# Attention scores by products over 64 rows, a tile's two key halves side by side on the two row halves of TensorE

## Chip, cores and metric

The kernel runs on one core of one Trainium2 chip. The metric is the device time of one execution in microseconds (us); lower is better. TensorE (PE in the profile) multiplies matrices into PSUM, its weight loads are listed as PEld, VectorE is DVE, ScalarE is ACT, GpSimd is POOL, and SyncE (SP) issues nearly all DMAs here.

## What is computed

Attention over 2 batches of 8 heads, 576 positions, 64 numbers per head, then two expert layers on the 1152 token rows of 512 numbers:

```python
q_rot, k_rot = (rotate(q), rotate(k))               # rotary embedding on both
scores = scale * np.matmul(q_rot, k_rot.transpose(0, 1, 3, 2))
scores = scores - np.max(scores, axis=-1, keepdims=True)
attn = np.exp(scores)
attn = attn / (np.sum(attn, axis=-1, keepdims=True) + 1e-09)
return np.matmul(attn, v).astype(np.float32)
# then x = heads side by side, (1152, 512)
x = elu(x @ w_in) @ w_out          # 512 -> 2048 -> 512
x = (h * tanh(softplus(h))) @ w2_out   where h = x @ w2_in
```

## The kernel before

**Numbers in two parts.** Products are made in the fp32r format. Each factor is split into a high part (`qh`, `kh`, ...) and the rest (`ql`, `kl`, ...), and a product is the sum of three: high by high, low by high, high by low.

**Attention.** The 16 heads are worked as 8 pairs (`p`); a pair's two heads lie on partitions 0 to 63 and 64 to 127. A pair has 9 units (`u = 9 p + i`). Units 0 to 7 are a tile each: one head `h`, 128 queries `t`. Unit 8 takes the last 64 queries of both heads at once, with block-diagonal weights `bh`, `bl` over all 128 rows. A unit's 576 scores lie in two PSUM banks, 288 keys (`HS`) in each (`j` = 0, 1).

`do_S(u)` makes the scores, `do_max` their extreme on DVE, `do_exp` the exponentials `P` on ACT. Three units later (`LAG`) `do_T` transposes `P` on PE into `psT`, 128x128 each (L481), with the leftover columns going into `psL` (L486, L483); DVE or ACT copies them to `pt`. `do_av` multiplies by the values with weights of 64 columns (L521, into `psA`). `do_spread` (L458, L462) turns the row sums on PE. There are two score buffers (`ps_s`), so a unit's scores wait for `do_exp` of two units before.

**Scores, first and second pair (`p < FLAT`).** Two units, one of each head, go together: a head's rows 0 to 63 or 64 to 127 alone are contracted (forms "64\*128 64x288" in the profile), three passes by two key halves by two heads, 12 matmuls, with the two heads' alternating.

**Scores, third to eighth pair.** A tile contracts all 128 rows. `ka` holds a head's high keys on rows 0 to 63 and low keys on rows 64 to 127; `qa` holds the high queries on both halves, `qb` the low queries on rows 0 to 63 and zeros below. `qa` by `ka` and `qb` by `ka`, for two key halves, are four matmuls "128\*128 128x288". `spread` makes these stacked tiles by DMAs on SP's queue from `kh`, `kl`, `qh`, `ql`, one pair ahead.

**Order.** The order of the work is written out by hand in one loop over `u`. In units 0 to 8 of a pair, what PE does right before `do_S` is: unit 0 `psL`; 1 `do_av`; 2 `psL`; 3 `do_spread` (L458, L462); 4 `do_av`; 5 `psL`; 6 `do_av`; 7 `do_spread` (L458); 8 `do_av`. Right behind `do_S` come the transposes `psT` of unit `u - 3`. Preparation of pair `p + 1` (rotation, splitting on POOL, the DMAs of `stack_k` and `stack_q`) is spread over pair `p`'s units; in the last two pairs, parts of the expert layers' weight preparation (L96 to L127) stand between the units.

**Expert layers.** `g1_mm` (L187) multiplies by the first weights, L777 and L801 by the second; the weights are turned from 64-bit floats to high and low parts on POOL, DVE and ACT as they come in.

Of the kernel before, what the change touches and what calls it, by code (L numbers as in the profile page):

```python
# [11 lines left out]
F32R = mybir.dt.float32r  # L12
# [9 lines left out]
def plain(ap):  # L22
    return ap.bitcast(F32)
# [3 lines left out]
def kernel(  # L27
# [11 lines left out]
    nc = tc.nc  # L39
    NP = qk.shape[0]  # L40
    S = qk.shape[3]
    HS = S // 2
# [11 lines left out]
    TPP = 9  # L54
# [118 lines left out]
    def ps_s():  # L173
        i = s_count[0]
        s_count[0] += 1
        if s_more[0] is not None and i % 3 == 2:
            return s_more[0].tile([128, 2, 512], F32, tag="s2", name="ps_s2", bufs=1)
        return s_pool.tile([128, 2, 512], F32, tag="s", name="ps_s", bufs=2)
# [67 lines left out]
    def attention(att, ps, tail):  # L246
# [11 lines left out]
        FLAT = 2  # L258
# [48 lines left out]

        def split_alloc(p):
            d = {}
            for nm in ("kh", "kl", "ql"):  # L310
                d[nm] = att.tile([128, S], F32R, tag=nm, name=nm, bufs=2)
            for nm in ("qa",) if p < FLAT else ("ka", "qa"):
                d[nm] = att.tile([128, 2, S], F32R, tag=nm, name=nm, bufs=2)
            d["qh"] = d["qa"][:, 0, :] if p < FLAT else att.tile([128, S], F32R, tag="qh", name="qh", bufs=1)
            i = p % 2
            d["qb"] = qb[i]
            d["bh"], d["bl"] = bd[i]
            sp_t[p] = d

        def split_half(p, i, h, l):  # L320
# [26 lines left out]
                in1=plain(d[h][:, cs]), op0=ALU.mult, op1=ALU.subtract,  # L347
            )

        def spread(dst, src, r):  # L350
            for h in range(2):
                nc.sync.dma_start(out=plain(dst[64 * r:64 * r + 64, h, :]), in_=plain(src[64 * h:64 * h + 64, :]))

        def stack_k(p):
            d = sp_t[p]
            spread(d["ka"], d["kh"], 0)
            spread(d["ka"], d["kl"], 1)

        def stack_q(p):
            d = sp_t[p]  # L360
            for r in range(0 if p < FLAT else 2):
                spread(d["qa"], d["qh"], r)
            if p >= FLAT:
                spread(d["qb"], d["ql"], 0)
            for r in range(2):
                sl = slice(64 * r, 64 * r + 64)
                nc.sync.dma_start(out=plain(d["bh"][sl, 64 * r:64 * r + 64]), in_=plain(d["qh"][sl, S - 64:S]))
                nc.sync.dma_start(out=plain(d["bl"][sl, 64 * r:64 * r + 64]), in_=plain(d["ql"][sl, S - 64:S]))

        tiles = [(h, t) for t in range(4) for h in range(2)] + [None]  # L370
        psS = {}
# [8 lines left out]
        def do_S(u):  # L380
            p, i = divmod(u, TPP)
            d = sp_t[p]
            if p < FLAT and i < TPP - 1:
                us = (u, u + 1) if i % 2 == 0 else ()
            else:
                us = (u,)
            work = []
            for w in us:
                psS[w] = ps_s()
                if tiles[w % TPP] is None:  # L390
                    work.append([
                        (d["bh"], lambda ks: d["kh"][:, ks]),
                        (d["bh"], lambda ks: d["kl"][:, ks]),
                        (d["bl"], lambda ks: d["kh"][:, ks]),
                    ])
                    continue
                h, t = tiles[w % TPP]
                cols = slice(128 * t, 128 * t + 128)
                if p < FLAT:
                    rows = slice(64 * h, 64 * h + 64)  # L400
                    work.append([
                        (d["qh"][rows, cols], lambda ks, rows=rows: d["kh"][rows, ks]),
                        (d["ql"][rows, cols], lambda ks, rows=rows: d["kh"][rows, ks]),
                        (d["qh"][rows, cols], lambda ks, rows=rows: d["kl"][rows, ks]),
                    ])
                else:
                    work.append([
                        (d["qa"][:, h, cols], lambda ks: d["ka"][:, h, ks]),
                        (d["qb"][:, h, cols], lambda ks: d["ka"][:, h, ks]),
                    ])  # L410
            for a in range(len(work[0]) if work else 0):
                for j in range(2):
                    for w, passes in zip(us, work):
                        l, r = passes[a]
                        nc.tensor.matmul(  # L415
                            psS[w][:, j, :HS], lhsT=l, rhs=r(slice(j * HS, j * HS + HS)),
                            start=(a == 0), stop=(a == len(passes) - 1),
                        )

        def do_max(u):  # L420
            m = att.tile([128, 16], F32, tag="mn", name="mn", bufs=4)[:, 0:1]
# [142 lines left out]
        bd = []  # L564
        for i in range(2):
            pair = []
            for nm in ("bh", "bl"):
                t = att.tile([128, 128], F32R, name=f"{nm}{i}")
                nc.vector.memset(plain(t), 0.0)
                pair.append(t)  # L570
            bd.append(pair)
        qb = [att.tile([128, 2, S], F32R, name=f"qb{i}") for i in range(2)]
        for t in sums:
            nc.vector.memset(t[:, :, 1:2], 1e-9)
        nc.vector.memset(pl_t[1][S - 512:128, 256:384], 0.0)
        for t in qb:
            nc.gpsimd.memset(plain(t[64:128]), 0.0)
        nc.gpsimd.memset(halves, 0.0)
        for h in range(2):
            nc.gpsimd.memset(halves[64 * h:64 * h + 64, 64 * h:64 * h + 64], 1.0)  # L580
        nc.gpsimd.tensor_tensor(out=twice, in0=idn[:, 0:64], in1=idn[:, 64:128], op=ALU.add)
        split_alloc(0)
        def keep_warm(n):
            for _ in range(n):
# [19 lines left out]
        def prepare(p, k):  # L604
            if k == 0:
                if p == 2:
                    load_pair(3)
                split_alloc(p)
                split_half(p, 2, "kh", "kl")
                stack_k(p)  # L610
            elif k == 1:
                split_half(p, 0, "qh", "ql")
                stack_q(p)
            elif p + 1 < NP:
                rope_part(p + 1, 2 if k < 5 else 0, (k - 2) % 3, nc.gpsimd)
# [26 lines left out]
        for u in range(max(av_at) + 1):  # L642
            p, i = divmod(u, TPP)
# [3 lines left out]
            if u == 2:  # L647
                load_pair(2)
                split_alloc(1)
# [17 lines left out]
            if u < NU:  # L667
                do_S(u)
# [16 lines left out]
            if u == 2:  # L685
                first_lo(*HEAD[-1])
                stack_q(0)
# [20 lines left out]
            if 0 <= u - LAG < NU:  # L708
                j = (u - LAG) % TPP
# [21 lines left out]
            if u == 7:  # L731
                stack_q(1)
# [176 lines left out]
    with tc.tile_pool(name="att", bufs=1, reuse_waits="tile") as att, tc.tile_pool(  # L909
        name="ps_att", bufs=1, space=bass.MemoryType.PSUM, reuse_waits="tile"  # L910
    ) as ps:
        with tc.manual_schedule():
            attention(att, ps, tail)
# [56 lines left out]
```

## Time and profile before

| | us |
|---|---|
| median of 3 runs | 559.64 |
| lowest and highest run | 558.6, 561.39 |
| span of the profiled execution, first to last instruction | 559.2 |

The profiled execution's own time outside its span is not listed; its span is 0.4 below the median of the runs. Attention lies in the first 160 us, the third to eighth pair's scores between 47.6 and 144.5 us of it. Times of the views are microseconds from the span's start. Matmuls are pipelined: one takes about 0.3 us from its start to its end, and the next one starts well before that, so that the distance of two starts is what one costs.

### The profile page before, as it was taken

Reading aid. Unit: us, or ns where it says so; the run is one execution under the profiler, and the core shown is the slowest. Engines: PE = TensorE matmul, PEld = TensorE weight load, DVE = VectorE, ACT = ScalarE, POOL = GpSimd, SP = SyncE. Lnnn points to the kernel's source line nnn. Section 1 sums busy time; section 2 is a strip of 40 time slices with the busy share of each in tenths; the row PEclk is TensorE's granted clock in tenths of the full one; section 3 lists DMA queues with packets and bytes.
Section 4 is the critical chain, followed back from the end, with each engine's and each line's share of the span. In section 5 each row is a group of like instructions: output and inputs, shape, how many; then the busy total and the mean of one; then the engine's idle time right before and its main releaser. Section 6 shows DMA issues by size and latency. Waiting matters only on the chain.

```text
span 559.2 us, 8818 instructions
## 1 busy us (share of the span) xinstructions
PE 546.1 (98%) x3328; PEld 500.5 (90%) x3328; DVE 375.8 (67%) x560; ACT 267.4 (48%) x459; POOL 244.4 (44%) x227
## 2 busy tenths in 40 slices
PE   7889999999999999999999999999999999999997
PEld 6667878888898999999999999999989989989985
DVE  4868777879867888888889878857336555521221
ACT  3746666677656675554554556344342233132120
POOL 7979898953315434434334531534414433310000
PEclk9979999999999999999999999999999999999999
DMA  7379778764331333323232321423222131000012
GB/s 234 106 208 222 184 207 215 198 140 144 88 114 42 113 113 111 112 78 93 96 112 76 114 76 38 139 88 114 84 105 90 62 114 43 34 0 1 38 39 94
DMA packets 49258, 59.82 MB, mean 107 GB/s; under 512 B 20928, under 2 KB 39104, under 8 KB 48448
## 3 DMA queue, kind: packets, MB, share of 16 engines
q1 hardware_dynamic: 48672, 58.67, 35.6%
q8 instruction: 26, 0.43, 0.3%
q10 hardware_dynamic: 544, 0.59, 0.3%
q14 instruction: 16, 0.13, 0.1%
HBM read 47.51 MB, written 2.36 MB: 89 GB/s over the span
## 4 chain that ended last, share of the span: by engine, by line
PE 87%; DVE 3%; POOL 3%; issue 3%; DMA 2%; ACT 1%; SPq 0%; POOLq 0%; ACTq 0%
PE ps_s L187 33%; PE ps_h L801 18%; PE ps_g L777 17%; PE ps_s L415 7%; PE psA L521 7%; PE psT L481 4%; DMA qk_t<-in_qk_dram 1%; DVE mn L422 1%; DMA bh<-qa 1%; ACT P L435 1%; POOL wu L96 1%; POOL wo0bl L127 1%; POOL wo0l L127 1%; PE psL L486 0%; DVE wu L108 0%
## 5 line engine op out<-in xcount | busy, mean ns | idle before, releaser
L100 DVE TENSOR_SCALAR wu<-wu 128x512 int32<-128x512 int32 x64 | 39.7, 620 | 43.1 <-POOL wu L96 43.1
L759 ACT ACTIVATE ta<-ps_s 128x768 f32<-128x768 f32 x24 | 19.5, 812 | 100.8 <-PE ps_s L187 100.8
L422 DVE TENSOR_REDUCE mn<-ps_s 128x1 f32<-128x576 f32 x72 | 53.5, 752 | 21.0 <-PE ps_s L415 20.8
L435 ACT ACTIVATE P<-ps_s,mn 128x576 f32<-128x576 f32 x72 | 53.1, 740 | 14.7 <-DVE mn L422 14.3
L104 DVE SCALAR_TENSOR_TENSOR wu<-raw,wu 128x512 int32<-128x512 int32 x64 | 50.6, 791 | 2.0
L187 PE MATMUL ps_s<-XH,wi0h 128*128 128x384 f32 x192 | 49.1, 336 | 0.0
L108 DVE SCALAR_TENSOR_TENSOR wu<-raw,wu 128x512 int32<-128x512 int32 x64 | 47.8, 747 | 1.8
L187 PE MATMUL ps_s<-XL,wi1h 128*128 128x384 f32 x192 | 48.9, 335 | 0.0
L187 PE MATMUL ps_s<-XL,wi0h 128*128 128x384 f32 x192 | 48.8, 335 | 0.0
L187 PE MATMUL ps_s<-XH,wi1l 128*128 128x384 f32 x192 | 48.8, 335 | 0.0
L187 PE MATMUL ps_s<-XH,wi0l 128*128 128x384 f32 x192 | 48.8, 335 | 0.0
L187 PE MATMUL ps_s<-XH,wi1h 128*128 128x384 f32 x192 | 48.7, 334 | 0.0
L96 POOL TENSOR_SCALAR wu<-raw 128x512 f32<-128x512 f32 x64 | 46.4, 728 | 4.3
L127 POOL TENSOR_TENSOR wi0l<-wu,wi0h 128x512 fp32r<-128x512 f32 x16 | 23.0, 1440 | 57.5 <-ACT wi0h L126 57.5
L127 POOL TENSOR_TENSOR wi1l<-wu,wi1h 128x512 fp32r<-128x512 f32 x16 | 24.3, 1523 | 54.1 <-ACT wi1h L126 54.1
L127 POOL TENSOR_TENSOR wo1l<-wu,wo1h 128x512 fp32r<-128x512 f32 x16 | 23.3, 1462 | 48.6 <-ACT wo1h L126 48.6
L481 PE MATMUL psT<-idn,P 128*128 128x128 f32 x288 | 43.7, 276 | 0.0
L761 DVE TENSOR_TENSOR g<-ta,g 128x768 fp32r<-128x768 f32 x16 | 17.5, 1093 | 37.0 <-ACT g L760 37.0
L501 ACT ACTIVATE pt<-psT 128x512 f32<-128x512 f32 x44 | 26.2, 597 | 28.9 <-PE psT L481 28.9
L521 PE MATMUL psA<-pt,v_t 128*64 128x256 f32 (+1 forms) x240 | 37.1, 410 | 2.3 <-DVE pt L499 1.8
L481 PEld LDWEIGHTS psT<-idn,P 128*128 128x128 f32 x288 | 35.2, 143 | 2.0 <-issue 1.4
L187 PEld LDWEIGHTS ps_s<-XH,wi0h 128*128 128x128 f32 x192 | 34.7, 188 | 1.4 <-issue 0.8
(177 smaller groups left out, 1370.1 us busy)
## 6 DMA issues: line engine op xcount, KB each, us to landing
raw<-in_w_in_dram SPq DMA_DIRECT2D x32, 512.0 KB, 3.7
raw<-in_w_out_dram SPq DMA_DIRECT2D x32, 512.0 KB, 3.2
qk_t<-in_qk_dram SPq DMA_DIRECT2D x6, 1152.0 KB, 5.5
qa<-qh SPq DMA_DIRECT2D x24, 144.0 KB, 2.7
out_dram<-Y SPq DMA_DIRECT2D x9, 256.0 KB, 2.0
ka<-kh SPq DMA_DIRECT2D x12, 144.0 KB, 3.1
ka<-kl SPq DMA_DIRECT2D x12, 144.0 KB, 3.0
qb<-ql SPq DMA_DIRECT2D x12, 144.0 KB, 2.7
```

The lines of the kernel that those rows point to most:

```text
L96: nc.gpsimd.tensor_scalar(out=u, in0=high.bitcast(F32), scalar1=REBASE, scalar2=0.0, op0=ALU.mult, op1=ALU.add)
L100: nc.vector.tensor_scalar(out=ui, in0=ui, scalar1=3, scalar2=0x7FFFFFF8, op0=ALU.logical_shift_left, op1=ALU.bitwise_and)
L104: nc.vector.scalar_tensor_tensor(out=ui, in0=high, scalar=-0x80000000, in1=ui, op0=ALU.bitwise_and, op1=ALU.bitwise_or)
L108: nc.vector.scalar_tensor_tensor(out=ui, in0=low, scalar=29, in1=ui, op0=ALU.logical_shift_right, op1=ALU.bitwise_or)
L127: nc.gpsimd.tensor_tensor(out=lo, in0=u, in1=plain(hi), op=ALU.subtract)
L187: nc.tensor.matmul(o[:, j, :CH], lhsT=ws[j][i][:, cc, :], rhs=x[:, cc, t * CH:t * CH + CH], start=(k == 0), stop=(k == 3 * NC - 1),)
L422: nc.vector.tensor_reduce(out=m, in_=psS[u][:, :, :HS], axis=AX.XY, op=ALU.min)
L435: nc.scalar.activation(out=P.rearrange("p (j n) -> p j n", j=2), in_=psS.pop(u)[:, :, :HS], func=AF.Exp, scale=-1.0, bias=mn_t.pop(u), acc ...
L481: nc.tensor.transpose(tv[:, c, :], P[:, k:k + 128], idn)
L521: nc.tensor.matmul(o[64 * h:64 * h + 64, cols], lhsT=v, rhs=rhs, start=(c == 0 and first), stop=(c == 4), skip_group_check=True,)
L777: nc.tensor.matmul(o[:, j, :CH], lhsT=WO[f][w][:, e * 128:e * 128 + 128], rhs=g_part(f, t, i), start=(k == 0), stop=(k == 3 * GF - 1),)
L801: nc.tensor.matmul(o, lhsT=l, rhs=w, start=(k == 0), stop=(k == 3 * GF - 1))
```

## The change

The third to eighth pair's tiles contract 64 rows, as in the first two pairs, but one tile at a time: key half 0 runs on rows 0 to 63 and key half 1 on rows 64 to 127. A head lies on one row half only, so the other half comes from copies with the two heads' rows exchanged: `qx` (high and low queries, whole) and `kx` (high and low keys, only the key half that is read there). A tile is six matmuls of "64\*128 64x288" instead of four of "128\*128 128x288", the row halves alternating. Of the DMAs of a pair, 10 copies of 64 rows by 576 numbers become 4 of 64 by 576 and 4 of 64 by 288; the four small ones for `bh` and `bl` stay. Tiles `ka`, `qa`, `qb` and the clearing of `qb` on POOL go; `qh` becomes a tile with two buffers for all pairs. Unit 8 and the first two pairs issue the same matmuls as before.

```diff
@@ split_alloc
-            for nm in ("kh", "kl", "ql"):
+            for nm in ("kh", "kl", "qh", "ql"):
                 d[nm] = att.tile([128, S], F32R, tag=nm, name=nm, bufs=2)
-            for nm in ("qa",) if p < FLAT else ("ka", "qa"):
-                d[nm] = att.tile([128, 2, S], F32R, tag=nm, name=nm, bufs=2)
-            d["qh"] = d["qa"][:, 0, :] if p < FLAT else att.tile([128, S], F32R, tag="qh", name="qh", bufs=1)
-            i = p % 2
-            d["qb"] = qb[i]
-            d["bh"], d["bl"] = bd[i]
+            if p >= FLAT:
+                d["qx"] = att.tile([128, 2, S], F32R, tag="qx", name="qx", bufs=2)
+                d["kx"] = att.tile([128, 2, HS], F32R, tag="kx", name="kx", bufs=2)
+            d["bh"], d["bl"] = bd[p % 2]
@@ copies
-        def spread(dst, src, r):
-            for h in range(2):
-                nc.sync.dma_start(out=plain(dst[64 * r:64 * r + 64, h, :]), in_=plain(src[64 * h:64 * h + 64, :]))
+        def swap(dst, src, cut):
+            for r in range(2):
+                c = slice(r * HS, r * HS + HS) if cut else slice(0, S)
+                nc.sync.dma_start(out=plain(dst[64 * r:64 * r + 64]), in_=plain(src[64 - 64 * r:128 - 64 * r, c]))
@@ stack_k
-            spread(d["ka"], d["kh"], 0)
-            spread(d["ka"], d["kl"], 1)
+            for n, nm in enumerate(("kh", "kl")):
+                swap(d["kx"][:, n, :], d[nm], True)
@@ stack_q
-            for r in range(0 if p < FLAT else 2):
-                spread(d["qa"], d["qh"], r)
-            if p >= FLAT:
-                spread(d["qb"], d["ql"], 0)
+            for n, nm in enumerate(("qh", "ql") if p >= FLAT else ()):
+                swap(d["qx"][:, n, :], d[nm], False)
@@ do_S
-                if p < FLAT:
...
-                else:
-                    work.append([
-                        (d["qa"][:, h, cols], lambda ks: d["ka"][:, h, ks]),
-                        (d["qb"][:, h, cols], lambda ks: d["ka"][:, h, ks]),
-                    ])
-            for a in range(len(work[0]) if work else 0):
-                for j in range(2):
-                    for w, passes in zip(us, work):
...
+            def native(nm, n, rows, cs):
+                return d[nm][rows, cs]
+
+            def swapped(nm, n, rows, cs):
+                return d["qx"][rows, n, cs] if nm[0] == "q" else d["kx"][rows, n, :]
+
+            def product(w, j, at, rows, cols):
+                ks = slice(j * HS, j * HS + HS)
+                q, k = [[at(x + y, n, rows, c) for n, y in enumerate("hl")] for x, c in (("q", cols), ("k", ks))]
+                work.append((w, j, ((q[0], k[0]), (q[1], k[0]), (q[0], k[1]))))
...
+                    h, t = tiles[w % TPP]
+                    r = h if p < FLAT else j
+                    product(
+                        w, j, native if r == h else swapped,
+                        slice(64 * r, 64 * r + 64), slice(128 * t, 128 * t + 128),
+                    )
+            if p < FLAT:
+                work.sort(key=lambda x: x[1])
+            for a in range(3):
+                for w, j, passes in work:
+                    nc.tensor.matmul(
+                        psS[w][:, j, :HS], lhsT=passes[a][0], rhs=passes[a][1], start=(a == 0), stop=(a == 2),
+                    )
@@ attention, before the loop
-        qb = [att.tile([128, 2, S], F32R, name=f"qb{i}") for i in range(2)]
-        for t in qb:
-            nc.gpsimd.memset(plain(t[64:128]), 0.0)
```

## Rows read from the trace of the kernel before

**Rows 1.** The page: PE's busy time; the chain that ended last

```profile
PE 546.1 (98%) x3328; PEld 500.5 (90%) x3328; DVE 375.8 (67%) x560; ACT 267.4 (48%) x459; POOL 244.4 (44%) x227
PE 87%; DVE 3%; POOL 3%; issue 3%; DMA 2%; ACT 1%; SPq 0%; POOLq 0%; ACTq 0%
```

**Rows 2.** Busy time of the engines in two stretches, with PE's granted clock

```profile
30.00:40.00 10.00, 7.70 (x49) 5.30 (x47) 4.55 (x8) 4.34 (x12) 6.00 (x6) 0.68 0.85 235
...
80.00:90.00 10.00, 10.00 (x83) 8.54 (x82) 7.82 (x16) 6.49 (x17) 8.57 (x9) 1.00 0.89 199
```

**Rows 3.** The chain in order of time: unit 1 of two pairs

```profile
83.45 0.73 PE ps_s L415 x4
...
99.98 0.73 PE ps_s L415 x4
```

**Rows 4.** Timeline of PE: units 4 and 5 of a later pair

```profile
88.44 0.54 PE L415 MATMUL ps_s<-ka,qa 128*128 128x288 f32 x2
...
89.09 0.60 PE L481 MATMUL psT<-idn,P 128*128 128x128 f32 x4
89.52 0.27 PE L486 MATMUL psL<-idn,P 128*128 128x128 f32 x1
...
90.17 0.60 PE L481 MATMUL psT<-idn,P 128*128 128x128 f32 x4
```

**Rows 5.** Timeline of PE: two groups of twelve in the second pair

```profile
27.54 0.53 PE L415 MATMUL ps_s<-kh,qa 64*128 64x288 f32 x4
...
29.02 0.27 PE L486 MATMUL psL<-idn,P 128*128 128x128 f32 x1
...
43.00 0.27 PE L486 MATMUL psL<-idn,P 128*128 128x128 f32 x1
...
43.57 0.43 PE L415 MATMUL ps_s<-kh,ql 64*128 64x288 f32 x4
43.83 0.44 PE L415 MATMUL ps_s<-kl,qa 64*128 64x288 f32 x4
...
44.48 0.27 PE L481 MATMUL psT<-idn,P 128*128 128x128 f32 x1
```

**Rows 6.** Timeline of PE's weight loads, around both kinds of scores

```profile
43.20 0.30 PEld L415 LDWEIGHTS ps_s<-kh,qa 64*128 64x128 f32 x4 [0.17 <-issue]
...
44.20 0.20 PEld L458 LDWEIGHTS psA<-idn,R 128*128 128x128 f32 x2 [0.17 <-issue]
...
89.53 0.30 PEld L415 LDWEIGHTS ps_s<-ka,qa 128*128 128x128 f32 x2
```

**Rows 7.** Timeline around unit 3 of a later pair, ACT and PE

```profile
85.77 0.20 ACT L435 ACTIVATION_READ_ACCUMULATOR P<-ps_s,mn 128x1 f32 x1
...
85.86 0.33 PE L462 MATMUL psA<-R,halves 128*128 128x64 f32 x2
...
86.67 0.60 PE L481 MATMUL psT<-idn,P 128*128 128x128 f32 x4
87.20 0.48 PE L521 MATMUL psA<-pt,v_t 128*64 128x320 f32 x1
```

**Rows 8.** Timeline of PE behind unit 7 of the eighth pair

```profile
144.47 0.60 PE L481 MATMUL psT<-idn,P 128*128 128x128 f32 x4
145.23 0.43 PE L521 MATMUL psA<-pt,v_t 128*64 128x256 f32 x1 [0.17 <-ACT R L466]
```

**Rows 9.** Timeline of PE where the expert layers begin

```profile
176.69 0.62 PE L777 MATMUL ps_g<-ge,wo0bl 128*128 128x384 f32 x2 [0.81 <-POOL wo0bl L127]
```

**Rows 10.** The page: the DMAs that make `qa`

```profile
qa<-qh SPq DMA_DIRECT2D x24, 144.0 KB, 2.7
```

**Rows 11.** Timeline of POOL before the first scores

```profile
1.38 2.05 POOL L577 MEMSET qb<- 64x1152 f32 x2
...
7.20 0.66 POOL L298 TENSOR_TENSOR qk_t<-qk_t,tab 128x128 f32<-128x128 f32 x1 [2.71 <-DMA qk_t<-in_qk_dram]
```

**Rows 12.** Timeline of PE where its clock falls, second pair

```profile
34.58 0.77 PE L521 MATMUL psA<-pt,v_t 128*64 128x320 f32 x1 [1.80 <-DVE pt L499]
```

More of the change, by code (lines that the diff above doesn't have):

```diff
@@ L388, in do_S @@
             for w in us:
                 psS[w] = ps_s()
-                if tiles[w % TPP] is None:
-                    work.append([
-                        (d["bh"], lambda ks: d["kh"][:, ks]),
-                        (d["bh"], lambda ks: d["kl"][:, ks]),
-                        (d["bl"], lambda ks: d["kh"][:, ks]),
-                    ])
-                    continue
-                h, t = tiles[w % TPP]
-                cols = slice(128 * t, 128 * t + 128)
-                if p < FLAT:
[L400 to L405, printed above, removed]
-                else:
-                    work.append([
-                        (d["qa"][:, h, cols], lambda ks: d["ka"][:, h, ks]),
-                        (d["qb"][:, h, cols], lambda ks: d["ka"][:, h, ks]),
-                    ])
@@ L411, in do_S @@
-            for a in range(len(work[0]) if work else 0):
-                for j in range(2):
-                    for w, passes in zip(us, work):
[L414 to L418, printed above, removed]
+                for j in range(2):
+                    if tiles[w % TPP] is None:
+                        k = [d[nm][:, j * HS:j * HS + HS] for nm in ("kh", "kl")]
+                        work.append((w, j, ((d["bh"], k[0]), (d["bh"], k[1]), (d["bl"], k[0]))))
+                        continue
+                    h, t = tiles[w % TPP]
[4 more added lines that the diff above has]
+                    )
```

## The prediction

> **What bounds the kernel now.** I read the page first: TensorE is busy for 98% of the span and the chain that ended last is 87% TensorE [rows 1]. Such a share is an average over stages, so I went to the stage that the change touches, the third to eighth pair. In the table of stretches PE is busy for all of 80 to 90 us at the full clock, with DVE at 78% and ACT at 65% [rows 2]. The chain in order of time shows the same: unit 1 of one pair comes 16.53 us after that of the pair before, and what lies between is nearly all PE [rows 3]. So a nanosecond that a unit gains or loses on PE moves everything after it, save where PE waits for something.
>
> What a unit costs is read from starts in the timeline. The four transposes of a unit take 89.52 - 89.09 = 0.43 us, 0.11 each [rows 4]. A tile's scores of now, four matmuls over 128 rows, lie between `psL` at 89.52 and the transposes at 90.17: 0.65, less 0.11 for `psL`, is 0.54 us, four slots of 0.134 [rows 4]. The weight load of the scores starts at 89.53, under `psL`, with no idle time before it [rows 6]: the step from transposes to scores and back costs nothing.
>
> **What the change removes.** The first two pairs already run the form that comes. There, four matmuls of 64 rows start within 43.83 - 43.57 = 0.26 us [rows 5]: two on different row halves share a slot of 0.132, and each has its own weight load in it. So six matmuls of a tile are three slots, 0.40 us, where now there are 0.54: 0.14 less per tile. With 8 tiles in each of 6 pairs, 48 tiles, that is 6.5 us less, if nothing is added.
>
> **What it adds on TensorE.** The same rows show what lies around a group of 64-row matmuls. The weight loads before it and behind it each follow 0.17 us of idle time that no semaphore explains [rows 6]: the array is emptied between 128-row work and 64-row work, and the first load, which else hides under the matmuls before, is exposed. I take the sum from two whole groups of twelve (two tiles, six slots), so that nothing depends on how a matmul's end is modelled.
>
> Ahead of the group stands 128-row work: from `psL` at 43.00 to the transposes at 44.48 are 1.48 us [rows 5]. Less `psL` (0.11) and the two transposes of `R` between (0.22), 1.15 are left for twelve matmuls and both changes of form. Six matmuls are three slots fewer, 1.15 - 0.40 = 0.75. Against 0.54 now: **0.21 more** for such a tile.
>
> Ahead of the group stands `do_av`, whose weights have 64 columns: from 27.54 to `psL` at 29.02 are 1.48, four transposes included [rows 5]. Three slots fewer are 1.08. Now, unit 4, also behind `do_av`, takes 88.44 to 89.52, the same 1.08 [rows 4]. **No difference**: the change of form ahead of the tile is paid already, and what the three slots save goes into the one behind it.
>
> By the hand-written order units 1, 4 and 6 follow `do_av`, and units 0, 2, 3, 5 and 7 follow 128-row work. Behind every one come the transposes. Unit 3 is special. Two small products of `R` begin at 85.86 and the transposes behind the scores at 86.67, 0.81 later; at the rates above, 0.12 and 0.54 are 0.66. PE waits for the other 0.15 until ACT has read unit 1's score buffer (that read ends at 85.97) [rows 7]. Unit 2 is then 0.21 later already, so this wait goes, and unit 3 adds 0.06. A pair: 4 x 0.21 + 0.06 + 3 x 0 = 0.90 us, and six pairs 5.4 us.
>
> One rule of the Trainium skill speaks against the change as well: TensorEngine Tiling (Array Packing), Key Properties, says that a change of the tiling mode drains TensorE. It names no price and nothing of a weight load. The rows would price the drain alone at 43.20 - 43.00 - 0.11 = 0.09 us ahead of a group [rows 5, 6]; with as much behind it, units behind 128-row work would take 0.40 + 0.18 for 0.54, those behind `do_av` 0.05 less than now, and six pairs come out at +0.3 us, no change. The whole groups of rows 5 show more than that, and I go by them.
>
> **What takes some of it up.** In the seventh and eighth pair `do_av` behind unit 7 waits: the transposes start at 144.47 and `do_av` at 145.23, 0.76 later, where 0.53 is usual (86.67 to 87.20) [rows 7, 8]. It waits for ACT's copy of `R`, whose transposes stand before unit 7, so unit 7's 0.21 is hidden there: 2 x 0.21 = -0.4. Where the expert layers begin, PE waits 0.81 us for prepared weights [rows 9]. That preparation is partly paced by its own engines and may catch up: between 0 and -0.8, I take -0.4, as its pieces stand in order behind attention's work on the same engines.
>
> **What I cost at nothing.** The copies: 10 of 144 KB per pair become 4 of that size and 4 of half. They land in about 2.7 us [rows 10], are issued in units 0 and 1 and first read a pair later, some 16 us on; fewer can't be later. If this cover were gone, unit 0 would wait those 2.7 us. POOL's clearing of `qb`, 2.05 us, ends at 3.4 and POOL then idles 2.71 until a load lands [rows 11], so its removal frees nothing. Later reads of `qh` and `ql` by the scores hold their buffers longer, but `kh` and `kl` are held as long now, through unit 8. Unit 8 and the first two pairs keep their matmuls. DVE and ACT wait for PE in this stage and get slower work, not more.
>
> **Sum.** 5.4 - 0.4 - 0.4 = +4.6 us on the profiled execution's span of 559.2, 563.8. That span is 0.4 below the median of the runs, 559.64, what lies around it being unknown: **564.2 us**. A change of less than 0.5% (2.8 us) can't be told from none here: 556.8 to 562.4 is "same".
>
> **Rivals.**
>
> *The row halves win.* A tile costs its three slots and nothing for entering or leaving the form: the 6.5 us above, less what unit 3 then waits longer for ACT: about 553, faster. It decides once the changes of form around a tile cost less together than the 0.14 that it saves. For it: the slots are shared as hoped [rows 5]. Against it: both gaps of 0.17 [rows 6], and the 1.15 for a group of twelve. Chance 0.08. The Trainium skill has it so: TensorE: Matmul & The Clock Gate, Part 3, gives packed matmuls the time of one plus about 4 ns for each further one, with nothing for entering the form. The trace agrees as to the shared slot and not as to the rest.
>
> *The changes of form cost only their drain, or are hidden by waits.* About 560. For it: one tile's loads are fewer than a double group's and could be fetched sooner. Against it: rows 5 and 6 have the same first pair of loads. Chance 0.12.
>
> *The clock.* In 30 to 40 us the granted clock averages 0.68 [rows 2], after PE stood idle for 1.80 us behind DVE [rows 12]. A mean of 0.68 between the levels 0.5 (1.2 GHz) and 1 (2.4 GHz) is 6.4 us of the ten at the lower one, work that takes 3.2 at the upper. The change leaves that work as it is, but if fewer copies or a shifted start let the clock stand, 3.2 of the 4.6 us come back: 561. Chance 0.10.
>
> *The halves of one tile don't share slots.* In rows 5 the alternating matmuls write two tiles; the new ones write two banks of one. Three more slots per tile would be 48 x 0.40 = 19 us, about 583. Against it: two banks are what each tile has now, too. Chance 0.04.
>
> **Chances.** My forecast, PE longer by the changes of form, has 0.62; its own range is 562.4 to 566.5. The rest, 0.04, is for a lower clock in the stage from the emptier array, up to 570. Slower: 0.62 + 0.04 + 0.04 and a little of the second rival, 0.71; same: most of the second and the third, 0.20; faster: 0.09. The range takes in the second and third rival, and above, 0.5 us per pair more than forecast: 560 to 567.
>
> **What the profile would show.** In the timeline, pairs of 64-row matmuls starting within about 15 ns, three slots of 0.13; idle time of PEld near 0.17 before and behind each tile; from `psL` to the transposes behind a tile 0.80 where there were 0.65, and those four transposes 0.06 longer than 0.43; behind `do_av`, scores and transposes together an unchanged 1.08; a pair's period 17.4 instead of 16.5. I am wrong if `psL` to transposes stays at 0.65 or below, or if the period grows and the start of the expert layers doesn't.

## The result, and the profile after

The changed kernel takes 566.12 us (median of 4 runs, 565.13 to 567.73); in the same session the kernel before took 559.12 (4 runs). The ratio is 1.0118, 95% interval 1.009 to 1.0147: slower by about 1%. A second comparison, on another occasion, gave 565.94 us and 1.0109 (1.0084 to 1.0134). The profiled execution has a span of 565.0 us where there were 559.2, and took 566.76, so 1.76 us lie around its span.

The page of the changed kernel, PE's busy time and the chain, to be held against [rows 1]; 98% and 87% are the same figures on a longer span:

```profile
PE 552.2 (98%) x3424; PEld 494.6 (88%) x3424; DVE 375.9 (67%) x560; ACT 267.6 (47%) x459; POOL 242.1 (43%) x225
PE 87%; DVE 3%; POOL 3%; issue 3%; DMA 2%; ACT 1%; SPq 0%; POOLq 0%; ACTq 0%
```

The table of stretches, columns as in [rows 2]. In 80 to 90 us PE is still busy throughout, the share of DMA has fallen from 0.89 to 0.54, and none of PE's waits there is for a DMA:

```profile
30.00:40.00 10.00, 7.70 (x49) 5.27 (x47) 4.64 (x8) 4.43 (x12) 9.44 (x8) 0.70 0.76 225
80.00:90.00 10.00, 10.00 (x85) 7.23 (x85) 7.60 (x15) 7.31 (x19) 6.67 (x8) 1.00 0.54 125
```

The chain in order of time, unit 1 of two pairs as in [rows 3]. The period is 17.54 us where it was 16.53:

```profile
85.84 0.59 PE ps_s L414 x6
...
103.38 0.59 PE ps_s L414 x6
```

The timeline of PE over units 4 and 5, the same stretch of a pair as [rows 4]:

```profile
91.17 0.40 PE L414 MATMUL ps_s<-kh,qh 64*128 64x288 f32 x1
...
91.76 0.66 PE L479 MATMUL psT<-idn,P 128*128 128x128 f32 x4
92.25 0.27 PE L484 MATMUL psL<-idn,P 128*128 128x128 f32 x1
92.46 0.40 PE L414 MATMUL ps_s<-kx,qx 64*128 64x288 f32 x1
92.46 0.40 PE L414 MATMUL ps_s<-kh,qh 64*128 64x288 f32 x1
92.69 0.30 PE L414 MATMUL ps_s<-kx,qx 64*128 64x288 f32 x1
92.70 0.29 PE L414 MATMUL ps_s<-kh,ql 64*128 64x288 f32 x1
92.83 0.29 PE L414 MATMUL ps_s<-kx,qx 64*128 64x288 f32 x1
92.83 0.29 PE L414 MATMUL ps_s<-kl,qh 64*128 64x288 f32 x1
93.05 0.66 PE L479 MATMUL psT<-idn,P 128*128 128x128 f32 x4
```

The six matmuls start in twos, the second of them within 0.01 us of the first: native and exchanged rows share a slot, and the second and third slot lie 0.14 apart. But from `psL` at 92.25 to the first score are 0.21 us, where `psL` alone needs 0.11; the first slot lasts 0.23 instead of 0.13; and the transposes begin 0.22 after the last slot. `psL` to transposes is 0.80 instead of 0.65, and the four transposes take 92.25 - 91.76 = 0.49 instead of 0.43. Unit 4, behind `do_av`, is unchanged with its transposes: 91.17 to 92.25, 1.08.

The weight loads stand idle at such a step as they do in [rows 6], here behind unit 4's tile and ahead of unit 5's:

```profile
91.76 0.42 PEld L479 LDWEIGHTS psT<-idn,P 128*128 128x128 f32 x4 [0.16 <-issue]
...
92.45 0.18 PEld L414 LDWEIGHTS ps_s<-kx,qx 64*128 64x128 f32 x1 [0.17 <-issue]
```

No run separates what of this is the matmuls running out and what the load that no longer hides under them; the whole price is measured below.

### The profile page after: what moved, and what is told of

Same layout as the page of the kernel before. It is cut to its first block, busy times and chain, and to the rows that moved or that the text cites. A ratio compares the mean times of both kernels' runs of the same rounds, so it can differ in the third digit from the quotient of the medians.

```text
span 565.0 us, 8984 instructions
## 1 busy us (share of the span) xinstructions
PE 552.2 (98%) x3424; PEld 494.6 (88%) x3424; DVE 375.9 (67%) x560; ACT 267.6 (47%) x459; POOL 242.1 (43%) x225
## 4 chain that ended last, share of the span: by engine, by line
PE 87%; DVE 3%; POOL 3%; issue 3%; DMA 2%; ACT 1%; SPq 0%; POOLq 0%; ACTq 0%
PE ps_s L187 32%; PE ps_h L796 17%; PE ps_g L772 17%; PE ps_s L414 7%; PE psA L519 7%; PE psT L479 6%; DMA qk_t<-in_qk_dram 1%; DMA bh<-qh 1%; DVE mn L420 1%; ACT P L433 1%; POOL wu L96 1%; POOL wo0bl L127 1%; POOL wo0l L127 1%; PE psL L484 1%; PE psA L456 0%
## 5 line engine op out<-in xcount | busy, mean ns | idle before, releaser
L479 PE MATMUL psT<-idn,P 128*128 128x128 f32 x288 | 46.7, 287 | 0.0
L479 PEld LDWEIGHTS psT<-idn,P 128*128 128x128 f32 x288 | 31.8, 143 | 9.9 <-issue 7.4
```

What stands on the lines that cost most here:

```text
L479: nc.tensor.transpose(tv[:, c, :], P[:, k:k + 128], idn)
```

## The experiments

Theory A is the prediction's: TensorE changes its form on the way into and out of every tile, and that costs more than the slot saved. Rivals: B, the copies; C, six matmuls and loads instead of four cost as such; D, the two halves of one tile do not share slots. All times are medians, and ratios are to the kernel before, run beside them.

**The copies left out** (both halves read the heads' own rows):

```diff
-                        w, j, native if r == h else swapped,
+                        w, j, native,
...
-            for n, nm in enumerate(("kh", "kl")):
+            for n, nm in enumerate(()):
...
-            for n, nm in enumerate(("qh", "ql") if p >= FLAT else ()):
+            for n, nm in enumerate(()):
```

> The changed kernel without its eight copies per pair (qx and kx are neither allocated nor filled): both key halves' matmuls read the heads' own rows, so a tile's second half contracts the other head's numbers. Same matmuls, same forms, same order. Theory A (the array changes its form twice per tile, which costs more than the saved slot): the copies are hidden, time stays at that of the changed kernel, 565 to 567 us, a pair's period stays at 17.54 us. Rival B (the copies with exchanged rows, or waits on them, make it slower): back to 560 us or below.

Measured: 565.7 us, ratio 1.0082 (1.0064 to 1.01). The chain in order of time, `do_av` behind unit 0 of two pairs:

```profile
101.12 1.45 PE psA L519 x12
118.64 1.45 PE psA L519 x12
```

The period is 17.52 us. B falls: neither the copies nor waits on them are the loss.

**A pass left out:**

```diff
-                work.append((w, j, ((q[0], k[0]), (q[1], k[0]), (q[0], k[1]))))
+                work.append((w, j, ((q[0], k[0]), (q[1], k[0]), (q[0], k[1]))[:3 if p < FLAT else 2]))
...
```

> The changed kernel with the third pass (high queries by low keys) left out in the third to eighth pair's tiles: four matmuls of 64 rows, two shared slots, in place of six. Theory A: one slot of 0.13 us goes from each of 48 tiles and nothing else, 6.3 us less than the changed kernel, 560 us: no faster than the kernel before, though it does two thirds of the tile's work. Rival C (the six instructions and six weight loads cost, not the change of form): four against four of before, at half the rows each, 546 to 553 us.

Measured: 558.43 us, ratio 0.9972 (0.9954 to 0.9989). With a third of a tile's products gone, the gain over the kernel before is 0.3%, and not all of that is the kernel's: at a mean granted clock of 0.999 or more it took 558.2 to 558.9 us and the kernel before 558.4 to 560.5. The timeline of PE ahead of and behind unit 5, then the chain's period:

```profile
86.87 0.27 PE L485 MATMUL psL<-idn,P 128*128 128x128 f32 x1
...
87.54 0.44 PE L480 MATMUL psT<-idn,P 128*128 128x128 f32 x2
```

```profile
79.55 1.45 PE psA L520 x12
96.02 1.45 PE psA L520 x12
```

`psL` to transposes is 0.67 with two slots, 0.13 less than with three and still above the 0.65 of before; the period is 16.47 against 16.53. Two slots and the changes of form cost about what four full slots cost. C, which expected 546 to 553, falls.

**Six matmuls over all 128 rows** (each sums both heads' scores):

```diff
-                        w, j, native if r == h else swapped,
-                        slice(64 * r, 64 * r + 64), slice(128 * t, 128 * t + 128),
+                        w, j, native,
+                        slice(64 * r, 64 * r + 64) if p < FLAT else slice(0, 128), slice(128 * t, 128 * t + 128),
```

> The changed kernel with the six matmuls of a tile in the third to eighth pair contracting all 128 rows (both heads' scores added up), on the heads' own tiles; copies still made, not read. The form never changes between scores and transposes. Theory A: six slots of 0.134 us and no empty array, 0.27 us more per tile than before less what unit 3 waits for ACT now: a pair's period 18.5 us, 570 us. From the transposes back to scores no idle weight load. Rival C (six loads and matmuls are what costs): as the changed kernel, 566 us.

Measured: 571.88 us, ratio 1.0191 (1.0166 to 1.0215). The timeline of PE and of its weight loads around a tile behind `psL`:

```profile
84.54 0.27 PE L484 MATMUL psL<-idn,P 128*128 128x128 f32 x1
...
85.46 0.60 PE L479 MATMUL psT<-idn,P 128*128 128x128 f32 x4
```

```profile
84.54 0.30 PEld L414 LDWEIGHTS ps_s<-kh,qh 128*128 128x128 f32 x2
```

0.92 us less `psL`'s 0.11 are six slots of 0.135, and the load follows without idle time. So a tile of six full slots takes 0.81 and the changed kernel's three shared slots take 0.75, counted as in the prediction, behind 128-row work: the three slots saved are 0.40, and the changes of form take back 0.35 of it there.

**The change of form put into the kernel before** (the left-out rows of `qb` are zeros, so that the two matmuls of `qb` run in the 64-row form):

```diff
-                        (d["qb"][:, h, cols], lambda ks: d["ka"][:, h, ks]),
+                        (d["qb"][0:64, h, cols], lambda ks: d["ka"][0:64, h, ks]),
```

> The kernel before, where the two matmuls of qb by ka in the third to eighth pair's tiles contract rows 0 to 63 alone; rows 64 to 127 of qb are zeros, so the sums are the same. Four matmuls on four slots as before, but the array changes its form between the second and third and again behind the fourth. Theory A: 0.35 us more per tile (0.20 ahead, 0.16 behind), less 0.15 per pair that unit 3 waits now and 0.5 in the last pairs: about +15 us, 574 us. If a change costs its drain alone (0.09 at each side): +8, 567 us. Rival C (the count of instructions): as before, 559 us.

Measured: 574.46 us, ratio 1.0242 (1.0222 to 1.0262), with the same number of matmuls, loads and slots as before. The timeline of PE and of its loads around one tile:

```profile
83.55 0.27 PE L486 MATMUL psL<-idn,P 128*128 128x128 f32 x1
83.57 0.51 PE L415 MATMUL ps_s<-ka,qa 128*128 128x288 f32 x2
84.01 0.53 PE L415 MATMUL ps_s<-ka,qb 64*128 64x288 f32 x2
84.47 0.66 PE L481 MATMUL psT<-idn,P 128*128 128x128 f32 x4
```

```profile
83.55 0.30 PEld L415 LDWEIGHTS ps_s<-ka,qa 128*128 128x128 f32 x2
84.01 0.29 PEld L415 LDWEIGHTS ps_s<-ka,qb 64*128 64x128 f32 x2 [0.16 <-issue]
84.47 0.42 PEld L481 LDWEIGHTS psT<-idn,P 128*128 128x128 f32 x4 [0.16 <-issue]
```

`psL` to transposes is 0.92 instead of 0.65, plus 0.06 in the transposes: 0.33 us for a way in and a way out; the weight loads stand idle for 0.16 at each. This is the price by itself, and more than twice the 0.14 that a tile of the change saves. The case of a drain alone, 567 us, falls with it.

**One row half for both key halves** (no copies are made):

```diff
...
-                    r = h if p < FLAT else j
+                    r = h
```

> The changed kernel, but a tile's six matmuls in the third to eighth pair all run on the row half that holds the head, as no copies are needed then (none are made). Same count of matmuls, loads and changes of form; only the sharing of slots is gone. Theory A: six slots of 0.13 us in place of three, 0.40 more per tile, 48 tiles: 19 us more than the changed kernel, 583 to 585 us. Rival D (the halves of one tile, which write two banks of one buffer, do not share slots in the changed kernel either): no slower than it, 566 us.

Measured: 584.81 us, ratio 1.0445 (1.0424 to 1.0467). PE's timeline around a tile behind `psL`:

```profile
88.97 0.27 PE L484 MATMUL psL<-idn,P 128*128 128x128 f32 x1
...
90.16 0.66 PE L479 MATMUL psT<-idn,P 128*128 128x128 f32 x4
```

1.19 against 0.80: three slots more at 0.13, as the forms and their changes are the same. D falls; in the changed kernel the halves do share.

**Two tiles between changes of form, everywhere** (`FLAT = 8`, no copies):

> All eight pairs in the form of the first two: two tiles, one of each head, go together as twelve matmuls of 64 rows on the heads' own tiles, no copies with exchanged rows. Half as many changes of form. Theory A: 1.15 us of TensorE per two tiles, about 1 us less per pair than the changed kernel; but two tiles are asked of DVE and ACT at once with two score buffers, so TensorE may wait for them. Without waits 560 us, as before; with 0.3 to 1 us of waits per pair 562 to 566 us. Rival C (count of instructions): as the changed kernel or above.

Measured: 576.49 us, ratio 1.03 (1.0279 to 1.0321), far above what I allowed for waits. PE's timeline:

```profile
85.36 0.39 PE L414 MATMUL ps_s<-kh,qh 64*128 64x288 f32 x1
86.29 0.53 PE L414 MATMUL ps_s<-kh,qh 64*128 64x288 f32 x3 [0.54 <-ACT P L433]
```

A group has started its first tile and stands 0.9 us until ACT has read the second tile's buffer. Fewer changes of form are of no use here, where the tiles must then come in twos; this run says nothing on the price.

**Groups of two only where `do_av` has just changed the form** (in the kernel before, with `qh` in two buffers):

```diff
...
+            return {1: (u, u + 1), 4: (u, u + 1), 6: (u, u + 1), 2: (), 5: (), 7: ()}.get(i, (u,))
...
```

> The kernel before, where in the third to eighth pair units 1 and 2, 4 and 5, 6 and 7 go together in the 64-row form, each group right behind do_av, where the array has changed its form anyway; units 0 and 3 stay as before. Theory A: each group saves two times 0.137 us and pays one change of form behind it, 0.156: 0.12 less, three groups in six pairs 2.1 us less than before, unless TensorE waits for the score buffers: 0.3 us of waits per pair would eat it up. 557 to 561 us. Rival C: three groups of twelve instead of 24 instructions per pair make it slower by the same rate as the changed kernel, 4 us or more.

Measured: 566.24 us, ratio 1.0116 (1.0094 to 1.0137). My figure of 557 to 561 was wrong. PE's timeline behind units 1 and 2, and around units 6 and 7:

```profile
86.64 0.30 PE L486 MATMUL psL<-idn,P 128*64 128x128 f32 x1 [0.59 <-DVE pl L514]
...
93.54 0.53 PE L418 MATMUL ps_s<-kh,qh 64*128 64x288 f32 x4
...
94.52 0.66 PE L484 MATMUL psT<-idn,P 128*128 128x128 f32 x4
```

The group of units 6 and 7 shows the saving: 0.98 us up to the transposes, where the kernel before needs 0.65 for a tile behind `do_av` (88.44 to 89.09 in [rows 4]) and 0.54 for the other. With 0.06 more in the transposes it saves 0.15, where theory A had 0.12. The groups of units 1 and 2 (83.70 to 84.85) and 4 and 5 (89.53 to 90.61) take 1.15 and 1.08; why they take longer stays open.

At 86.64 PE waits because DVE takes both tiles' maxima ahead of emptying `psL`. So I took the second maximum out of the way:

```diff
-            for w in group(u):
+            for w in group(u) if p < FLAT else (u,):
                 if w < NU:
                     do_max(w)
```

> The kernel with groups of two tiles behind do_av, but the maximum of a group's second tile is taken on DVE in that tile's own unit, not right behind the first one's. In the run without this, TensorE waited 0.75 us per pair in unit 2 for psL, which DVE empties only after both maxima. Theory A with waits (the groups save 0.36 us per pair on TensorE, waits for the shared buffers cost more): that wait goes, six pairs 4.5 us less, 561 us, still no faster than before. If the form itself were the loss (rival C): as without this, 566 us.

Measured: 565.55 us, ratio 1.0098 (1.0075 to 1.012): wrong again. Who waited for whom in 47 to 145 us (us in total, times, longest):

```profile
PEld ps_s L418 <- ACT P L438: 4.1, 13, 0.6
...
PEld psA L524 <- ACT R L469: 2.3, 6, 0.4
...
PEld psL L486 <- DVE pl L514: 1.9, 6, 0.3
```

and the last of these rows without this edit:

```profile
PEld psL L486 <- DVE pl L514: 5.0, 6, 0.8
```

The wait for `psL` fell from 5.0 us to 1.9, but the period stayed at 17.48 (98.66 to 116.14 between two `do_av` of the chain): the tiles that come in twos wait for the score buffers, for `R` and for `psL` in turn. The waits and the longer groups outweigh what a group saves; how they share the 0.95 us per pair is not shown. No version here that makes all three products beats the kernel before.

**The changed kernel again:**

> The changed kernel once more, beside the next three on one chip. Theory A: a pair's period 17.54 us, 565 to 567 us, whether or not TensorE's clock falls in the second pair, where its records differ from run to run.

Measured: 565.94 us, and a period of 17.54 between the scores of two units 8 (81.36 to 98.90).

## Why the prediction was right, and by how much it was off

The forecast of 564.2 us came out at 566.1, on the forecast side and for the forecast reason, 0.4 below the upper end of the forecast's own range. Its steps:

- **A shared slot of 0.13, three of them**: right, by the timeline after and by the run on one row half.
- **0.21 for a tile behind 128-row work**: right, 0.15 up to the transposes and 0.06 in them. The price alone was 0.33 us per tile in the kernel before with 64-row products put in.
- **Nothing for a tile behind `do_av`**: right, 1.08 with its transposes as before.
- **Unit 3, 0.06**: small miss. There the profile now shows

```profile
88.48 0.33 PE L460 MATMUL psA<-R,halves 128*128 128x64 f32 x2
...
89.33 0.66 PE L479 MATMUL psT<-idn,P 128*128 128x128 f32 x4
```

  0.85, plus 0.06 in the transposes, against 0.81 [rows 7]: 0.10. The prediction put 0.12 on the two short products and 0.15 on the wait for ACT. In the run with groups of two, where unit 3 keeps its four matmuls and ACT is done in time, the same stretch is

```profile
87.00 0.33 PE L465 MATMUL psA<-R,halves 128*128 128x64 f32 x2
...
87.75 0.60 PE L484 MATMUL psT<-idn,P 128*128 128x128 f32 x4
```

  0.75, so the short products take 0.21 and the wait was 0.06. Both terms were mis-sized, and so was the change of form at this place, 0.91 - 0.75 = 0.16: what unit 3 adds is 0.16 - 0.06 = 0.10, where the prediction has 0.21 - 0.15 = 0.06. That these are close is luck. A pair costs 1.01 us instead of 0.90; unit 3 has 0.04 of this, the rest is spread over the others by 0.01 or 0.02 each.
- **The wait behind unit 7 in the last two pairs**: right. Transposes to `do_av` took 0.76 [rows 8] and now take 150.82 - 150.24 = 0.58:

```profile
150.24 0.66 PE L479 MATMUL psT<-idn,P 128*128 128x128 f32 x4
150.82 0.51 PE L519 MATMUL psA<-pt,v_t 128*64 128x256 f32 x2
```

- **0.4 us taken up where the expert layers begin**: wrong. The wait stands where it stood [rows 9]; the weight preparation moved along with attention:

```profile
182.31 0.62 PE L772 MATMUL ps_g<-ge,wo0bl 128*128 128x384 f32 x2 [0.83 <-POOL wo0bl L127]
```

- **Copies, `qb`, buffers at nothing**: the copies, right (565.7 us without them). For the others no run was made; the period, made up of PE's terms, leaves nothing for them.
- **The base**: the forecast adds 4.6 to the median of the kernel before, but the profiled execution of 559.2 was not a median one. All 40 executions of the two kernels whose span is on record took 1.7 to 1.9 us more than their spans, so this one took an estimated 561.0, 1.4 above the median of its three runs; the changed kernel's profiled execution lies 0.6 above its own. From one profile to the other, both with the clock down in the second pair (0.68 and 0.70 in 30 to 40 us), it is 5.8 us: the sum fell short by 1.2. The other 0.7 of the 1.9 comes from which executions were compared.

Where the 1.2 lie: the chain's unit 8 of the second pair, which the change leaves as it was, starts before and after at

```profile
46.32 1.00 PE ps_s L415 x6
```

```profile
46.59 0.99 PE ps_s L414 x6
```

From there to `do_av` behind the eighth pair's unit 7 are 98.91 us before (to 145.23 [rows 8]) and 104.23 after (to 150.82): 5.3 more, against 5.4 - 0.4 = 5.0 in the sum. To these 0.3 come the 0.4 that the expert layers did not take up, 0.3 ahead of the stretch and 0.2 behind 182.31; why the two profiles differ by the last two stays open.

The clock is in the medians as well. None of the eight executions of the changed kernel had a mean granted clock above 0.997; of the 32 of the kernel before that ran beside the experiments, nine had 0.999 or more. At 0.996 to 0.997 the medians differ by 5.1 us (565.3 and 560.2), at 0.988 to 0.994 by 5.7 (566.8 and 561.0). So the change costs 5 to 6 us, rather than the 7.0 between the medians of the first comparison. That the change makes the fall likelier is not shown: with a pass left out, five of nine executions had 0.999.

Of the rivals, no slot sharing and a drain alone fell to the runs above. The rival that the row halves win fell to the 0.33 us: its condition was a price under 0.14. The clock's rival did not come about in the changed kernel (0.70 in 30 to 40 us of its profile, 0.68 before), but other kernels of this record were profiled without the fall, below.

## What to carry to other kernels

Count a TensorE saving in slots, and then every place where neighbouring instructions differ in rows or columns used: here one way into and out of the 64-row form cost 0.33 us, two and a half slots of 288 columns, so a group has to save more than that before the switch pays. Behind `do_av`, where the kernel before pays a way in already (0.65 for the tile instead of 0.54), only the way out is new, and three slots in place of four just made up for it. Whole groups in the trace, from a plain instruction before to a plain one behind, gave this price within 0.02 us, where a drain read from a single gap would have called the change neutral. Grouping more work between two switches asks for buffers: here, with two score buffers, groups of two waited for DVE and ACT and came out slower than the kernel before in all three runs.

## What the runs showed of the hardware

The clock's fall in the second pair is not part of every execution of the same work. In the profile of the kernel before with 64-row products, PE stood idle as long behind the same copy as in [rows 12] (1.81 us), yet the granted clock stayed at the upper level, 2.4 GHz:

```profile
34.44 0.46 PE L521 MATMUL psA<-pt,v_t 128*64 128x320 f32 x1 [1.81 <-DVE pt L499]
```

```profile
30.00:40.00 10.00, 7.67 (x68) 5.51 (x67) 6.71 (x13) 5.62 (x16) 5.64 (x6) 1.00 0.89 234
```

Its third pair's scores start 2.5 us ahead of those of the kernel before, 0.1 of which it has from the start (first scores at 9.36 and 9.50 us), so the fall costs about 2.4 us. First this kernel, then the kernel before:

```profile
45.12 0.51 PE L415 MATMUL ps_s<-ka,qa 128*128 128x288 f32 x2
```

```profile
47.61 0.51 PE L415 MATMUL ps_s<-ka,qa 128*128 128x288 f32 x2
```

Over whole executions the 32 of the kernel before beside the experiments took 558.35 to 560.51 us at a mean clock of 0.999 or more and 560.66 to 562.34 at 0.994 or less. Why the clock falls in one execution and not in another stays open; for readers it means that two single profiles of such a kernel can differ by half a per cent with nothing changed, and that the sum has to be made on stages that both have at the same clock.
